# A third chunk's second group with its own place and bank, value rows added ahead of mean products, key copies ahead of maxima, and queries loaded later

## The chip, the cores and the metric

The kernel runs on one core of a Trainium2 chip. Its engines are TensorE (PE: products, with a separate queue of weight loads, PEld), VectorE (DVE), ScalarE (ACT), GpSimd (POOL) and SyncE (SP, which here only issues DMAs). The metric is the device time of one execution in microseconds (us), lower is better. A time is the median of several runs.

## The reference

Two layers in a row. The first is attention with a window: each query sees the keys less than 16 positions away, and beside them 24 block summaries (the maximum over each block of 32 keys, with the mean over the same 32 rows as its value). The second is a gated product with two up-projections and one down-projection.

```python
# q, k, v: (4, 8, 768, 64)   w_a, w_b: (512, 1536)   w_out: (1536, 512)
k_sum = k.reshape(B, H, nb, 32, D).max(axis=3)
v_sum = v.reshape(B, H, nb, 32, D).mean(axis=3)
scores_l = where(|i - j| < 16, scale * q @ k.T, -1e9)
scores_s = scale * q @ k_sum.T + log(32)
a = softmax(concat([scores_l, scores_s]))
x = (a @ concat([v, v_sum])) -> (3072, 512)
out = ((x @ w_a) * (x @ w_b)) @ w_out
```

## The kernel before

**Chunks, groups, items.** The 3072 rows are taken in 12 chunks of 256 (three per batch element), a chunk in two groups of 128 rows. For a group the kernel forms scores against 128 key columns per head (`scores`, L561), softmax, a transposition of the probabilities (`transposes`, L664) and the product with the values (`products`, L701), which is split into a high and a low part, `x` (L720 on ACT, L723 on DVE). An item (L937) is one chunk `u` and one block `f` of 128 of the 1536 hidden columns: 24 up-products into `h` (L932), four short operations on ACT and DVE (L949, L952, L954, L957), and 6 down-products into `o` (L968). There are 144 items. The first two chunks' items are interleaved, `(0,0) (0,1) (1,0) (0,2) (1,1) ...`, so that each block of weights is used twice while the weights are being prepared; from the third chunk on, the chunks follow one another.

**Weights.** The weights arrive as 36 raw parts, two to a pair `j` (0 to 17, tile `W{j}`), and `convert(j)` (L266) turns each into a high and a low part: per half of a pair ACT scales (L289) into bank `c0`, DVE runs three steps (L297, L304, L310) that use banks `c0` and `c1`, ACT makes the high part (L342), and POOL makes the low part with a subtraction and an addition (L347, L353). Pair `j`'s raw parts are loaded once pair `j - 4` is converted (`done{j-4}`). The last four pairs work in three half spaces that are taken in turn (`slots`, L264).

**The first two chunks** (`first_attention`, L742) have ways of their own: the keys are transposed by PE into four banks (`first_keys`, L417), ACT copies each to `kT` in two parts (L433 low, L435 high), DVE takes the block maxima (L443), POOL spreads them (`summaries`, L409). The block means of the values come from PE with a matrix of 1/32 (`means`, L822): six loaded pieces with two adjacent rows in each partition, two products for each piece.

**The third chunk** (`FILL`, attention(2), L856) is put between the conversions by three `yield`s. It shares `c0` and `c1` with them: `begin(0)` (query transposition L881, scores) comes after pair 9, `begin(1)` after pair 17. Both its groups put the transposed probabilities in `pbuf` (`pt`) and the value product in `c0`. Both use the same value rows `vbuf`, loaded by `bring`.

**Order.** Nothing is issued by hand. `Work.add` notes for each operation its engine, a rank, a guessed duration, and the keys that it reads and writes; `emit` (L50) plays the list against guessed times and issues, for the engine that is free first, the operation of lowest rank among those that are ready. The result is one fixed order for each engine, SP's loads included. Each engine works its order off one by one: what waits holds all behind it. Ranks: 0 for steps of an item on ACT and DVE, 1 for the first chunk, 2.3 for the second, `2 + j/4` for conversions, 5 for the third chunk, 5.5 for the next batch's keys, 6 for the rest.

**Spaces.** `S0` and `S1` hold 128x2048 each. Besides the conversions, `S0.0` and `S0.1` stage output rows, `S0.2` and `S0.3` hold the value sums of the next batch (`prep_values`, L497), `S1.0` and `S1.1` the value rows for them, `S1.2` and `S1.3` keys (`prep_keys`, L455).

Of the kernel before, what the change touches and what calls it, by code (L numbers as in the profile page):

```python
# [15 lines left out]
ALU = mybir.AluOpType  # L16
# [68 lines left out]
def attention_moe(  # L85
# [10 lines left out]
    nc = tc.nc  # L96
    B, H, S, D = q.shape
    P = 128
# [12 lines left out]
    CV = 512  # L111
    NW = 3 * NF // 2
    AHEAD = (7, 9, 17)
    FILL = 2

    const = ctx.enter_context(tc.tile_pool(name="const", bufs=1))
# [78 lines left out]
    for j in (*range(8, 13), *range(NW - 3, NW)):  # L195
        spaces[f"W{j}"] = wp.tile([P, 2048], F32, tag=f"W{j}", name=f"space{j}")

    kins = [kin, spaces["S1"][:, 2 * CV : 2 * CV + S + 32]]

    def slot(space, i):  # L200
# [12 lines left out]
    def act(rank, takes, reads, writes, fn):  # L213
        work.add("ACT", rank, takes, 0.08, reads, writes, fn)
# [46 lines left out]
            "SP", rank, 0.45, 524.0, [f"done{j - 4}"] if j > 3 else [], writes, fn, rate=340  # L261
        )

    slots = [("S0", 0), ("S0", 2), ("S1", 2)]  # L264

    def convert(j):  # L266
        rank = CONVERT + j / 4
        rk = [f"raw{2 * j}", f"raw{2 * j + 1}"]

        if j < NW - 4:  # L270
# [146 lines left out]
    def first_keys():  # L417
        n = P // BLK
        for i in range(S // P):
            x, key = spot(i // 2)  # L420
            x, key = x[:, i % 2 * 512 : (i % 2 + 1) * 512], key[i % 2]
            load(
                i, 262.0, 215, (), [key], x.rearrange("p (h d) -> p h d", d=D),
                heads(k[0, :, i * P : (i + 1) * P, :]),
            )
            bk = ("c0", "c1", "o2", "o3")[i % 4]
            pe(FIRST, 0.85, [key], [bk], lambda bk=bk, x=x: turn(bank[bk], x))
            c0 = PER * i

            def put(lo, bk=bk, c0=c0):  # L430
                tr = bank[bk].rearrange("p (c x) -> p c x", x=P)
                if lo:
                    nc.scalar.copy(out=kT[:, :, c0 + 16 : c0 + WIN], in_=tr[:, :, : WIN - 16])  # L433
                else:
                    nc.scalar.copy(  # L435
                        out=kT[:, :, c0 + P : c0 + PER + 16], in_=tr[:, :, WIN - 16 :]
                    )

            act(FIRST, 0.43, [bk], [f"kTl{i}"], lambda put=put: put(True))
            act(FIRST, 0.33, [bk], [f"kTh{i}"], lambda put=put: put(False))  # L440
            dve(
                FIRST, 0.6, [bk], [f"ksi{i}"],
                lambda bk=bk, i=i: nc.vector.tensor_reduce(  # L443
                    out=ks[:, :, i * n : (i + 1) * n],
                    in_=bank[bk].rearrange("p (c n x) -> p c n x", n=n, x=BLK),
                    axis=AX.X, op=ALU.max,
                ),
            )
        for c in range(NP):
            work.add("-", 0, 0, 0, [f"ksi{i}" for i in range(6)], [f"ks{c}"], lambda: None)  # L450
            reads = [f"kT{x}{i}" for i in range(6) for x in "lh"]
            work.add("-", 0, 0, 0, reads, [f"kT{c}k"], lambda: None)
            summaries(FIRST, c)

    def prep_keys(b):  # L455
# [91 lines left out]
    def load_values(b, t, vw, keys, rank):  # L547
        row = t * P
        skip = 16 if t == 0 else 0
        end = min(row + P + 16, S)  # L550
        for i, (e, r0, lo, hi) in enumerate((
            (0, skip, row - 16 + skip, row + 80),
            (1, 0, row + 48, row + 80),
            (1, 64, row + 80, end),
        )):
            load(
                rank, 2.1 * (hi - lo), 215, (), [keys[i]], vw[e][r0 : r0 + hi - lo],
                heads(v[b, :, lo:hi, :]),
            )

# [103 lines left out]
    def transposes(u, t, s, sk, banks, diag=None):  # L664
        rank = rank_of(u)
        if u < FILL:
            d, dk = diag

            def turned(h):
                for c in range(NP):  # L670
                    nc.tensor.matmul(
                        bank[banks[h]][:, c * P : (c + 1) * P], s[h][:, c, :], d[:, h, c, :],
                        start=True, stop=True,
                    )

            for h in range(2):
                pe(
                    -1, 0.85, [f"{sk[h]}{c}" for c in range(NP)] + dk[h], [banks[h]],
                    lambda h=h: turned(h),
                )  # L680
                act(
                    rank, 0.6, [banks[h]], dk[h],
                    lambda h=h: nc.scalar.copy(
                        out=d[:, h], in_=bank[banks[h]].rearrange("p (c x) -> p c x", x=P)
                    ),
                )
            return
        sv = sbuf.rearrange("p h c x -> p (h c) x")
        pv = pbuf.rearrange("p h c x -> p (h c) x")


        for i, kb in enumerate(((0, 1, 3), (1, 2, 3), (0, 1, 2), (1, 2, 3))):
            qs = slice(32 * i, 32 * (i + 1))
            for j in kb:
                js = slice(32 * j, 32 * (j + 1))
                dve(
                    rank, 0.45, sk, [f"pt{i}{j}"],
                    lambda js=js, qs=qs: nc.vector.transpose(out=pv[js, :, qs], in_=sv[qs, :, js]),  # L698
                )

# [36 lines left out]
    SK = ["s0", "s1"]  # L737
    PT = [f"pt{i}{j}" for i in range(4) for j in range(4)]

    PD = (pbuf, [[x for x in PT if (x[2] in "01") == (h == 0)] for h in range(2)])  # L740

    def first_attention():  # L742
# [78 lines left out]

        def means(n):  # L822
            g, i = n // 3, n % 3
            for y in range(2):
                nc.tensor.matmul(
                    bank["h0"][:, g * 256 : (g + 1) * 256], mean[:, 16 - 8 * i : 16 - 8 * i + P],
                    vin[n][0][:, :, y * D : (y + 1) * D],
                    start=(i == y == 0), stop=(i == 2 and y == 1),
                )

        for n in range(6):
            pe(FIRST + 0.5, 1.0, [vin[n][1], mk], ["h0"], lambda n=n: means(n))
        for e, r0 in ((0, WIN), (1, 32)):
            rows = slice(r0, r0 + 32)
            act(
# [20 lines left out]
    def attention(u):  # L856
# [1 line left out]
        b, r = u // NR, u % NR  # L858
        rank = rank_of(u)

        banks, vbank = [["c0", "c1"]] * 2, ["c0"] * 2
        if u > FILL:
            banks, vbank = [["c0", "c1"], ["o2", "o3"]], ["c0", "o2"]
        if r == 0:
# [2 lines left out]
        t0 = G * r  # L867
        qk = []
        for c in range(NP):
            qk += blocks(98, f"qin.{c}", qin[:, c, :], q, b, c, r * CH)  # L870

        def bring(i):
            load_values(b, t0 + i, vbuf, VK[:3], 97)
# [14 lines left out]
            transposes(u, t0 + i, s0, SK, banks[i])  # L888

        def end(i):  # L890
            return u, t0 + i, vbuf, VK, vbank[i]

        if u == FILL:

            yield
            bring(0)
            begin(0)
            turned(0)
            yield
            begin(1)  # L900
            yield
            values(*end(0))
            bring(1)
            turned(1)
            values(*end(1))
        elif u == FILL + 1:
            for i in range(G):
                bring(i)
                begin(i)
                turned(i)  # L910
                values(*end(i))
        else:

            for i in range(G):
                begin(i)
                bring(i)
                turned(i)
                lead.append(products(*end(i)))
# [128 lines left out]
```

## Time and profile before

| | |
|---|---|
| Median of 3 runs | 704.68 us (703.55 to 706.06) |
| Profiled execution | 704.12 us, span 702.4 us |
| Mean granted TensorE clock | 0.998 |
| Busy share of the span | PE 97%, PEld 89%, DVE 62%, ACT 36%, POOL 26% |
| Chain that ended last, by engine | PE 79%, DVE 7%, POOL 7%, issue 3%, ACT 2%, DMA 2% |
| HBM | 47.12 MB read, 6.29 MB written |

The span runs from the first to the last instruction; the execution's time has a little around it. A row of the timeline reads: start in us, length in us, engine, line of the kernel, operation, output<-input, shapes, count, and in brackets the idle time of the engine ahead of it with what ended it. A row of the table by stretches reads: the stretch and its length, then for each engine its busy time and (count), then PE's granted clock, the busy share of the DMA engines, and GB/s. `SPq` rows are DMA issues. A row of waits reads: engine and line that waited, for whom, total us, times, longest. Shares of busy time are averages over stretches with different limits, so they say little on a change to one stretch.

### The profile page before, as it was taken

How to read it: one execution, taken by the hardware profiler on the slowest of the kernel's cores; microseconds unless marked ns; L12 is line 12 of the kernel's file. 1: busy time of each engine (PE TensorE's matmuls, PEld its weight loads, DVE VectorE, ACT ScalarE, POOL GpSimd, SP SyncE). 2: the span in 40 equal slices, each digit the busy share in tenths (PEclk: the TensorE clock that was granted, in tenths of full speed). 3: DMA queues.
4: the chain of work that ended last, by engine and by line, in shares of the span. 5: the costliest groups of instructions: out<-in, count | busy, mean ns of one | idle time of the engine just before them, and what ended most of it. 6: DMA issues, size and time to landing. Idle time of an engine off the chain costs nothing.

```text
span 702.4 us, 15093 instructions
## 1 busy us (share of the span) xinstructions
PE 682.8 (97%) x6000; PEld 626.4 (89%) x6000; DVE 436.4 (62%) x988; ACT 252.4 (36%) x795; POOL 181.3 (26%) x219
## 2 busy tenths in 40 slices
PE   6888999999999999999999999999999999999997
PEld 3778999988999999999999999999999999999996
DVE  2898999797767777666763776762762662311221
ACT  2976574533333314332332323332331431211211
POOL 4378976852433521130110101110110110000000
PEclk9999999999999999999999999999999999999999
DMA  9979773076233335220300330310310100000000
GB/s 229 265 173 309 267 168 126 6 152 145 64 89 96 83 79 107 50 56 19 82 8 17 69 68 2 87 25 1 83 24 1 54 21 1 31 1 1 31 1 31
DMA packets 154943, 54.84 MB, mean 78 GB/s; under 512 B 132456, under 2 KB 147816, under 8 KB 154872
## 3 DMA queue, kind: packets, MB, share of 16 engines
q1 hardware_dynamic: 154872, 53.88, 31.5%
q8 instruction: 47, 0.77, 0.5%
q14 instruction: 24, 0.20, 0.1%
HBM read 47.12 MB, written 6.29 MB: 76 GB/s over the span
## 4 chain that ended last, share of the span: by engine, by line
PE 79%; DVE 7%; POOL 7%; issue 3%; ACT 2%; DMA 2%; SPq 0%; POOLq 0%; ACTq 0%; DVEq 0%
PE h L932 48%; PE o L968 24%; POOL w L353 3%; POOL S L347 2%; DVE c L304 2%; PE o L712 1%; PE c L712 1%; PE o L583 1%; PE c L583 1%; DVE space L297 1%; POOL space L347 1%; DVE space L310 1%; DMA raw<-in_moe_w_b_dram 1%; ACT s L628 1%; DVE ksum L443 1%
## 5 line engine op out<-in xcount | busy, mean ns | idle before, releaser
L932 PEld LDWEIGHTS h<-x,w 128*128 128x128 f32 x3456 | 416.0, 189 | 14.0 <-DVE x L723 2.2
L932 PE MATMUL h<-x,w 128*128 128x256 f32 x3456 | 419.4, 278 | 1.9 <-DVE x L723 1.7
L952 DVE TENSOR_TENSOR h<-h,g 128x256 f32<-128x256 f32 x144 | 62.2, 432 | 164.9 <-ACT g L949 163.2
L968 PE MATMUL o<-w,gh 128*128 128x512 f32 x576 | 157.8, 396 | 1.3 <-ACT gh L954 1.2
L949 ACT COPY g<-h 128x256 f32<-128x256 f32 x144 | 53.8, 374 | 280.8 <-PE h L932 279.9
L968 PEld LDWEIGHTS o<-w,gh 128*128 128x128 f32 x576 | 98.8, 188 | 18.6 <-ACT gh L954 2.3
L698 DVE STREAM_TRANSPOSE pt<-s 32x256 f32<-32x256 f32 x240 | 104.6, 436 | 8.7 <-POOL s L658 4.5
L658 POOL TENSOR_TENSOR s<-s,nml 128x512 f32<-128x512 f32 x40 | 41.6, 1042 | 257.0 <-DVE nml L643 255.5
L968 PE MATMUL o<-w,gl 128*128 128x512 f32 x288 | 90.1, 394 | 0.0
L957 DVE TENSOR_TENSOR gl<-h,gh 128x256 fp32r<-128x256 f32 x144 | 60.7, 422 | 31.6 <-ACT gh L954 30.2
L628 ACT ACTIVATE s<-s,nml 128x128 f32<-128x128 f32 x160 | 62.7, 398 | 43.3 <-DVE nml L616 43.3
L954 ACT CAST gh<-h 128x256 fp32r<-128x256 f32 x144 | 53.6, 372 | 67.6 <-DVE h L952 67.3
L968 PEld LDWEIGHTS o<-w,gl 128*128 128x128 f32 x288 | 53.8, 188 | 11.9 <-issue 0.3
L513 POOL TENSOR_TENSOR S<-S 96x512 f32<-96x512 f32 (+3 forms) x48 | 33.6, 699 | 39.1 <-DMA S<-in_v_dram 30.7
L347 POOL TENSOR_TENSOR space<-space,w 128x1024 f32<-128x1024 f32 (+1 forms) x13 | 26.7, 2056 | 18.8 <-ACT w L342 13.9
L628 ACT ACTIVATION_READ_ACCUMULATOR s<-s,nml 128x1 f32 x160 | 31.1, 194 | 0.0
L289 ACT ACTIVATE c<-raw 128x512 f32<-128x512 f32 x36 | 23.2, 644 | 13.2 <-DVE S L297 5.1
L353 POOL TENSOR_TENSOR w<-space 128x1024 fp32r<-128x1024 f32 (+1 forms) x13 | 26.8, 2059 | 0.9
L637 DVE TENSOR_SCALAR nml<-nml 128x4 f32<-128x4 f32 x40 | 9.8, 244 | 26.9 <-ACT s L628 26.9
L616 DVE TENSOR_REDUCE nml<-s 128x4 f32<-128x512 f32 x40 | 25.4, 669 | 0.0
L409 POOL COPY kT<-ksum 128x144 f32<-128x144 f32 x16 | 4.7, 308 | 61.5 <-DVE ksum L491 54.7
L347 POOL TENSOR_TENSOR S<-S,w 128x512 f32<-128x512 f32 (+1 forms) x11 | 17.6, 1598 | 9.7 <-ACT w L342 9.6
(100 smaller groups left out, 454.2 us busy)
## 6 DMA issues: line engine op xcount, KB each, us to landing
raw<-in_moe_w_a_dram SPq DMA_DIRECT2D x12, 512.0 KB
raw<-in_moe_w_b_dram SPq DMA_DIRECT2D x12, 512.0 KB
raw<-in_moe_w_out_dram SPq DMA_DIRECT2D x12, 512.0 KB
out_dram<-S SPq DMA_DIRECT2D x24, 256.0 KB
qin<-in_q_dram SPq DMA_DIRECT2D x160, 32.0 KB
S<-in_v_dram SPq DMA_DIRECT2D x24, 192.0 KB
vw<-in_v_dram SPq DMA_DIRECT2D x18, 192.0 KB
kin<-in_k_dram SPq DMA_DIRECT2D x24, 100.0 KB
```

Of the source, the lines that this page charges most:

```text
L347: lambda ms=ms, f8=f8: nc.gpsimd.tensor_tensor(out=f8, in0=f8, in1=parted(0)[:, ms].bitcast(F32), op=ALU.subtract),
L353: lambda ms=ms, f8=f8, p8=p8: nc.gpsimd.tensor_tensor(out=parted(1)[:, ms], in0=f8, in1=p8, op=ALU.add),
L513: lambda: nc.gpsimd.tensor_tensor(out=out, in0=i0, in1=i1, op=ALU.add),
L628: lambda h=h, c=c, sums=sums: nc.scalar.activation(s[h][:, c, :], x[h][:, c, :], AF.Exp, bias=m[:, 0, h, c : c + 1], scale=1.0, accum_out= ...
L658: lambda h=h, r=r: nc.gpsimd.tensor_tensor(out=s[h], in0=s[h], in1=r[:, :, None].broadcast_to([P, NP, P]), op=ALU.mult,),
L698: lambda js=js, qs=qs: nc.vector.transpose(out=pv[js, :, qs], in_=sv[qs, :, js]),
L932: nc.tensor.matmul(ps, w[:, c, part, :], x[xpart][:, c, :], start=(i == 0), stop=(i == n - 1))
L949: act(CHAIN, 0.38, [hk], [gk], lambda: nc.scalar.copy(out=g, in_=pa))
L952: lambda: nc.vector.tensor_tensor(out=pa, in0=pb, in1=g, op=ALU.mult),
L954: act(CHAIN, 0.41, [hk], [ghk], lambda: nc.scalar.copy(out=gh, in_=pa))
L957: lambda: nc.vector.tensor_tensor(out=gl, in0=pa, in1=gh.bitcast(F32), op=ALU.subtract),
L968: nc.tensor.matmul(bank[ok[j]], (gh if first else gl)[:, js], w[:, :, part, :], start=(f == 0 and first and part == 0), stop=(f == NF - 1 ...
```

## The change

1. `first_keys`: the two copies of a chunk of keys become one step of ACT, and DVE's maximum reads that step's key too, so it comes behind both copies.
2. `means`: POOL adds the two adjacent value rows of each piece in place, and PE takes one product for each piece instead of two.
3. The third chunk's query loads wait for `done4`.
4. The rank of `convert(j)` is `2 + j/6`. The three half spaces of the last four pairs are `S1.0`, `S0.0`, `S1.2` instead of `S0.0`, `S0.2`, `S1.2`.
5. The third chunk's second group puts its transposed probabilities in `S0.2` and `S0.3` (`pown`, cleared by POOL first) and its value product in `c1`; its transposes are entered ahead of the first group's value product, with rank 5, which is also the rank that the third chunk has.
6. The guessed rate of the value loads is 150 instead of 215; this changes only what `emit` plays with.

```diff
+    TURNS = 5
...
+    pown = spaces["S0"][:, 2 * CV :].rearrange("p (h c x) -> p h c x", h=2, x=P)
...
-    slots = [("S0", 0), ("S0", 2), ("S1", 2)]
+    slots = [("S1", 0), ("S0", 0), ("S1", 2)]
     def convert(j):
-        rank = CONVERT + j / 4
+        rank = CONVERT + j / 6
...
     # first_keys
-            act(FIRST, 0.43, [bk], [f"kTl{i}"], lambda put=put: put(True))
-            act(FIRST, 0.33, [bk], [f"kTh{i}"], lambda put=put: put(False))
+            act(FIRST, 0.75, [bk], [f"kT{i}"], put)
             dve(
-                FIRST, 0.6, [bk], [f"ksi{i}"],
+                FIRST, 0.6, [bk, f"kT{i}"], [f"ksi{i}"],
...
     # load_values
-                rank, 2.1 * (hi - lo), 215, (), [keys[i]], vw[e][r0 : r0 + hi - lo],
+                rank, 2.1 * (hi - lo), 150, (), [keys[i]], vw[e][r0 : r0 + hi - lo],
...
     # transposes
-        pv = pbuf.rearrange("p h c x -> p (h c) x")
+        own = u == FILL and t % G == 1
+        dst, key = (pown, "pu") if own else (pbuf, "pt")
+        pv = dst.rearrange("p h c x -> p (h c) x")
+        rank = TURNS if own else rank
...
-                    rank, 0.45, sk, [f"pt{i}{j}"],
+                    rank, 0.45, sk + ["S0.2"] * own, [f"{key}{i}{j}"],
...
     # first_attention
         def means(n):
             g, i = n // 3, n % 3
-            for y in range(2):
-                nc.tensor.matmul(
-                    bank["h0"][:, g * 256 : (g + 1) * 256], mean[:, 16 - 8 * i : 16 - 8 * i + P],
-                    vin[n][0][:, :, y * D : (y + 1) * D],
-                    start=(i == y == 0), stop=(i == 2 and y == 1),
-                )
+            nc.tensor.matmul(
+                bank["h0"][:, g * 256 : (g + 1) * 256], mean[:, 16 - 8 * i : 16 - 8 * i + P],
+                vin[n][0][:, :, :D], start=(i == 0), stop=(i == 2),
+            )
         for n in range(6):
-            pe(FIRST + 0.5, 1.0, [vin[n][1], mk], ["h0"], lambda n=n: means(n))
+            x, key = vin[n]
+            pool(
+                FIRST, 0.7, [], [key],
+                lambda x=x: nc.gpsimd.tensor_tensor(
+                    out=x[:, :, :D], in0=x[:, :, :D], in1=x[:, :, D:], op=ALU.add
+                ),
+            )
+            pe(FIRST + 0.5, 0.5, [key, mk], ["h0"], lambda n=n: means(n))
...
     # attention(u)
-        banks, vbank = [["c0", "c1"]] * 2, ["c0"] * 2
+        banks, vbank = [["c0", "c1"]] * 2, ["c0", "c1"] if u == FILL else ["c0"] * 2
...
-            qk += blocks(98, f"qin.{c}", qin[:, c, :], q, b, c, r * CH)
+            qk += blocks(98, f"qin.{c}", qin[:, c, :], q, b, c, r * CH, ["done4"] if u == FILL else ())
...
         def end(i):
-            return u, t0 + i, vbuf, VK, vbank[i]
+            pt = (pown, [PU, ["S0.2", "S0.3"]]) if u == FILL and i else None
+            return u, t0 + i, vbuf, VK, vbank[i], pt
...
             begin(1)
+            pool(rank, 0.9, (), ["S0.2", "S0.3"], lambda: nc.gpsimd.memset(pown, 0.0))
+            turned(1)
             yield
             values(*end(0))
             bring(1)
-            turned(1)
             values(*end(1))
```

More of the change, by code (lines that the diff above doesn't have):

```diff
@@ L428, in first_keys, with put @@
             c0 = PER * i
-            def put(lo, bk=bk, c0=c0):
+            def put(bk=bk, c0=c0):
                 tr = bank[bk].rearrange("p (c x) -> p c x", x=P)
[L432 to L436, printed above, removed]
-                    )
-            act(FIRST, 0.43, [bk], [f"kTl{i}"], lambda put=put: put(True))
-            act(FIRST, 0.33, [bk], [f"kTh{i}"], lambda put=put: put(False))
+                nc.scalar.copy(out=kT[:, :, c0 + 16 : c0 + WIN], in_=tr[:, :, : WIN - 16])
+                nc.scalar.copy(
+                    out=kT[:, :, c0 + P : c0 + PER + 16], in_=tr[:, :, WIN - 16 :]
+                )
+            act(FIRST, 0.75, [bk], [f"kT{i}"], put)
             dve(
-                FIRST, 0.6, [bk], [f"ksi{i}"],
+                FIRST, 0.6, [bk, f"kT{i}"], [f"ksi{i}"],
                 lambda bk=bk, i=i: nc.vector.tensor_reduce(
@@ L450, in first_keys @@
             work.add("-", 0, 0, 0, [f"ksi{i}" for i in range(6)], [f"ks{c}"], lambda: None)
-            reads = [f"kT{x}{i}" for i in range(6) for x in "lh"]
-            work.add("-", 0, 0, 0, reads, [f"kT{c}k"], lambda: None)
+            work.add("-", 0, 0, 0, [f"kT{i}" for i in range(6)], [f"kT{c}k"], lambda: None)
             summaries(FIRST, c)
@@ L738, in attention_moe @@
     PT = [f"pt{i}{j}" for i in range(4) for j in range(4)]
+    PU = [f"pu{i}{j}" for i in range(4) for j in range(4)]
     PD = (pbuf, [[x for x in PT if (x[2] in "01") == (h == 0)] for h in range(2)])
@@ L823, in means @@
             g, i = n // 3, n % 3
-            for y in range(2):
-                nc.tensor.matmul(
-                    bank["h0"][:, g * 256 : (g + 1) * 256], mean[:, 16 - 8 * i : 16 - 8 * i + P],
-                    vin[n][0][:, :, y * D : (y + 1) * D],
-                    start=(i == y == 0), stop=(i == 2 and y == 1),
-                )
-        for n in range(6):
-            pe(FIRST + 0.5, 1.0, [vin[n][1], mk], ["h0"], lambda n=n: means(n))
+            nc.tensor.matmul(
+                bank["h0"][:, g * 256 : (g + 1) * 256], mean[:, 16 - 8 * i : 16 - 8 * i + P],
+                vin[n][0][:, :, :D], start=(i == 0), stop=(i == 2),
+            )
+        for n in range(6):
+            x, key = vin[n]
[4 more added lines that the diff above has]
+                ),
+            )
+            pe(FIRST + 0.5, 0.5, [key, mk], ["h0"], lambda n=n: means(n))
         for e, r0 in ((0, WIN), (1, 32)):
```

## The prediction

> **What bounds the kernel now.** I read the page first (PE is busy nearly throughout), then the busy time of each engine in five stretches cut where the work changes: the first scores start at 18.32, the first expert products at 37.08, the second chunk's at 60.12, the third chunk's at 160.90.
>
> ```profile
> core 0: us, PE busy (x) PEld busy (x) DVE busy (x) ACT busy (x) POOL busy (x), PEclk, DMA share, GB/s
> 0.00:18.32 18.32, 10.64 (x41) 6.29 (x41) 5.12 (x8) 5.92 (x15) 9.05 (x57) 1.00 1.00 232
> 18.32:37.08 18.76, 17.55 (x229) 14.25 (x229) 16.49 (x32) 17.41 (x53) 7.20 (x8) 1.00 1.09 269
> 37.08:60.12 23.04, 19.80 (x197) 16.98 (x193) 20.21 (x41) 16.62 (x52) 16.23 (x11) 0.93 0.80 201
> 60.12:160.90 100.78, 97.61 (x788) 89.11 (x788) 93.45 (x184) 51.99 (x123) 76.73 (x48) 1.00 0.59 161
> 160.90:702.40 541.50, 537.24 (x4751) 499.76 (x4751) 301.17 (x727) 160.45 (x556) 72.05 (x97) 1.00 0.20 46
> ```
>
> After 160.90 PE is busy for 537.24 of 541.50 us: that stretch is PE's own work, and the change leaves it alone. So the time is the moment when the third chunk's products start, plus a constant 541.5, and only the first 160.9 us can move. In them PE stands idle for 7.68, 1.21, 3.24 and 3.17 us (length less busy), 15.3 in all. In the first stretch PE waits for keys. In the next two ACT and DVE are nearly full (17.41 and 16.49 of 18.76; 20.21 of 23.04 on DVE), so a chain of attention steps sets the pace; in the fourth PE and DVE (93.45 of 100.78) are both close to full.
>
> The chain in the first stretch is one of keys. Its rows in order of time, beginning with the first of six chunks of keys:
>
> ```profile
> 9.14 0.43 ACT L433 COPY kT<-c 128x320 f32<-128x320 f32 x1 [7.05 <-PE c L374]
> ...
> 9.60 0.69 DVE L443 TENSOR_REDUCE ksum<-c 128x16 f32<-128x512 f32 x1 [7.59 <-ACT kT L433]
> ...
> 10.32 0.32 ACT L435 COPY kT<-c 128x192 f32<-128x192 f32 x1 [0.76 <-DVE ksum L443]
> ...
> 16.63 0.69 DVE L443 TENSOR_REDUCE ksum<-c 128x16 f32<-128x512 f32 x1 [0.71 <-ACT kT L433]
> ...
> 17.38 1.05 POOL L409 COPY kT<-ksum 128x144 f32<-128x144 f32 x4 [6.80 <-DVE ksum L443]
> ```
>
> ACT's low copy, DVE's maximum and ACT's high copy take turns on one bank, so from the first maximum to the sixth a chunk costs (16.63 - 9.60) / 5 = 1.41 us, and POOL's key sums, then the scores at 18.32, wait for the sixth.
>
> The second thing is what holds up the second chunk, from the queue of SP, ACT, PE and POOL:
>
> ```profile
> 30.50 12.73 SPq L225 DMA_DIRECT2D qin<-in_q_dram  x16
> ...
> 52.86 0.61 SPq L254 DMA_DIRECT2D raw<-in_moe_w_b_dram  x1
> 54.23 1.04 PE L712 MATMUL o<-pt,vw 128*64 128x64 f32 x28 [0.66 <-DMA vw<-in_v_dram]
> 55.69 1.03 PE L712 MATMUL o<-space,space 128*64 128x64 f32 x28 [0.21 <-DMA space<-in_v_dram]
> 58.04 0.63 ACT L289 ACTIVATE c<-raw 128x512 f32<-128x512 f32 x1 [2.16 <-DMA raw<-in_moe_w_b_dram]
> 58.61 0.58 ACT L720 CAST x<-o 128x512 fp32r<-128x512 f32 x1
> 60.22 2.41 POOL L347 TENSOR_TENSOR space<-space,w 128x1024 f32<-128x1024 f32 x1 [2.43 <-ACT w L342]
> ```
>
> SP spends 12.73 us issuing the third chunk's queries, which nobody reads before 82.69 (below), and the raw weights stand behind them. One comes so late that ACT waits 2.16 us for it, with the second chunk's cast (L720, 58.61) queued behind that wait.
>
> The third thing is the end of the fourth stretch: what PE waited for in it, and the rows around the last conversions and the third chunk's second group.
>
> ```profile
> PE h L932 <- DVE x L723: 1.7, 2, 1.3
> PE o L968 <- ACT gh L954: 1.2, 2, 0.6
> ...
> PE h L932 <- POOL w L353: 0.2, 1, 0.2
> ...
> 82.69 0.70 DVE L881 STREAM_TRANSPOSE qT<-qin 128x512 f32<-128x512 f32 x1
> 109.84 1.77 DVE L698 STREAM_TRANSPOSE pt<-s 32x256 f32<-32x256 f32 x4
> 116.67 0.69 DVE L297 TENSOR_SCALAR S<-c 128x512 int32<-128x512 int32 x1
> 122.06 1.30 POOL L347 TENSOR_TENSOR S<-S,w 128x512 f32<-128x512 f32 x1 [6.04 <-ACT w L342]
> 141.44 1.15 PE L712 MATMUL c<-pt,vw 128*64 128x64 f32 x32 [0.35 <-DVE s L608]
> 146.70 1.04 POOL L658 TENSOR_TENSOR s<-s,nml 128x512 f32<-128x512 f32 x1 [0.40 <-DVE nml L643]
> 148.20 0.87 DVE L698 STREAM_TRANSPOSE pt<-s 32x256 f32<-32x256 f32 x2
> ```
>
> **The change, part by part.** Amounts are on the start of the third chunk's products; minus is a gain.
>
> *Key copies ahead of maxima.* Both copies now precede the maximum, so ACT copies chunk i+1 while DVE reduces chunk i. A chunk then costs the larger of 0.69 (DVE) and 0.43 + 0.32 = 0.75 (ACT): the six end near 9.14 + 6 x 0.75 + 0.69 = 14.3 instead of 16.63 + 0.69 = 17.32, a gain of 3.0. PE could follow by no more than 7.68 less the 4.47 us that it waits for its first mask, 3.2. DMA is full in both early stretches (share 1.00 and 1.09), so queries, values and raw weights need not come earlier with it: between 0 and -3.0 I take -2.5, nearer the chain's end because every wait in these rows is for ACT or DVE and none for a load.
>
> *Value rows added by POOL.* Twelve of 24 mean products go, and six additions of 128x256 come on POOL.
>
> ```profile
> 20.31 3.72 PE L825 MATMUL h<-space,space 128*128 128x256 f32 x16
> 29.72 1.28 POOL L347 TENSOR_TENSOR space<-space,w 128x512 f32<-128x512 f32 x1 [11.28 <-ACT w L342]
> L513 POOL TENSOR_TENSOR S<-S 96x256 f32<-96x256 f32 x3 | 2.2, 733 | 0.2
> ```
>
> PE is rid of 12 x 3.72 / 16 = 2.8 us, POOL gets 6 x 0.73 = 4.4 us inside an idle stretch of 11.28. PE is not what paces this stretch, so I take 0. Ends: -2.8, if PE were the pace, and +1.0, if POOL waits for a late value load with the key sums (1.05, 17.38) queued behind it. Without that cover the 4.4 would come in front of the first weight subtraction at 29.72.
>
> *Third queries loaded late.* They now wait for the conversion of weight pair 4, and SP goes straight on to raw weights and value rows. What goes: ACT's 2.16 wait, of which the cast at 58.61 gets 58.61 - (55.69 + 1.03) = 1.9 less about 0.2 of handing over, 1.7; and the value waits of 0.66 + 0.21. Together -2.5; ends 0 and the stretch's whole idle time, -3.24. The 16 issues (12.73 us) go into gaps between raw loads; DVE needs them by the time that takes 82.69 now. If they are later than that, DVE's in-order queue holds the conversions: rival 2.
>
> *Conversion rank j/6 instead of j/4.* Pairs 13 to 17 now go ahead of the third chunk's work on DVE and POOL. Before, twelve transposes and little else ran from 109.84 to 116.67 while pair 14 waited, and POOL idled for 6.04; so the last conversions come some 6 us earlier. By itself that saves only the 0.2 wait for L353, but without it PE could not keep an earlier start, since it meets the conversions there with no slack. The price: pairs 2 to 4 now rank level with or ahead of the second chunk's second group, and one conversion step of 0.69 in front of a reduction costs that: +0.7 (0 to +2.1 for three).
>
> *Own place and bank for the second group.* Its transposes began at 148.20, just after POOL's scaling (146.70 + 1.04 = 147.74), long after the first group's product had read the old place (141.44 + 1.15). So the own place removes no wait that is there: 0. What helps is that the scores behind it come with the conversions, 6 us earlier, and then x is no longer late at 160.90: -1.0 of the 1.3 in the first wait row (0 to -2.5 with the 1.2 for gh). The place is paid for by a clearing on POOL (a 128x512 operation is 1.28, so at most 2.6, in gaps) and by the value sums of the next batch, whose half of the space is held until the second group's product; these feed PE late:
>
> ```profile
> 189.83 1.15 PE L712 MATMUL c<-pt,vw 128*64 128x64 f32 x32
> ```
>
> That product serves the fourth chunk, after the third's twelve items; their up-products alone take 12 x 2.91 (106.18, below) = 35 us, so it is not needed before 160.9 + 35 = 195.8, and 6 us late costs 0.
>
> The other half of the space, S1.0, now takes part in the last conversions, so the next batch's value loads and POOL's first sums over them move behind the last conversion:
>
> ```profile
> 48.40 2.62 POOL L513 TENSOR_TENSOR S<-S 96x512 f32<-96x512 f32 x3 [0.46 <-DMA S<-in_v_dram]
> ```
>
> POOL is rid of 2.62 us there and has them later, in gaps: 0. The changed rate of the value loads only moves the planner's guess: 0.
>
> *Sum*: -2.5 + 0 - 2.5 + 0.7 - 1.0 = -5.3. The profiled execution took 704.12 us (span 702.4 and 1.72 around it): 698.8. The median of the runs is 704.68, 0.56 above it, so I predict 699.4.
>
> **A rule that speaks against it.** Where PE waited 2.02 us, its granted clock fell, and 24 products took longer than the 2.91 of the row at 106.18 below:
>
> ```profile
> 46.03 1.13 PE L671 MATMUL o<-pt,s 128*128 128x128 f32 x8 [2.02 <-ACT space L628]
> 46.91 4.61 PE L932 MATMUL h<-x,w 128*128 128x256 f32 x24
> 48.00:50.00 2.00, 2.00 (x12) 2.00 (x11) 1.90 (x6) 1.27 (x7) 1.52 (x2) 0.50 1.04 370
> ```
>
> That slow spell cost 4.61 - 2.91 = 1.7. The change thins PE's work by 2.8 us in the stretch before, so a second spell can come there: the sum would be -3.6, which is 701.1. The Trainium skill ("TensorE: Matmul & The Clock Gate", Part 1) says that the clock is halved after an idle window of about 3.4 us that runs freely and does not follow the kernel. By it the spell may come, go or stay by chance of position; the 0.50 row agrees with the half, no row here shows the window.
>
> **The rivals.**
> 1. *Conversions stay the pace.* PE arrives earlier at 60 but must wait for weights: POOL runs pair after pair at 2.41 + 2.41 us, and gets only the 2.43 wait at 60.22 back. Against it: pair 14's 6 us. Gain 2.0: 702.7.
> 2. *Queries too late: slower.* In order behind the raw loads, which SP issues until 75.5, the sixteen would be issued by 75.5 + 12.7 = 88.2 and land 1 to 5 us later (the raw load of 52.86 was there at 58.04, in a full DMA; I take 2 for these small ones): 90, and DVE's L881, in place at 82.69, would hold everything behind it 7.5 us. Part of that is covered by weights in hand (pair 11's end against its use):
>
> ```profile
> 100.12 2.41 POOL L353 TENSOR_TENSOR w<-S 128x1024 fp32r<-128x1024 f32 x1
> ...
> 106.18 2.91 PE L932 MATMUL h<-x,w 128*128 128x256 f32 x24
> ...
> 75.10 0.43 SPq L254 DMA_DIRECT2D raw<-in_moe_w_a_dram  x1
> ```
>
>  106.18 - 102.53 = 3.7. It decides from a hold of some 4 us on; at 7.5 PE ends 3.8 later: 708.5. For it: SP took 0.8 us for each, far more than a raw load's 0.43. Against: raw loads now start up to 12.7 us sooner and leave gaps.
> 3. *Nothing moves*: DMA, full until 37, paces the start and the queries' place only swaps waits: 704.7.
> 4. *All idle goes*: the second stretch's 1.2, the third's 3.24 with the 1.7 of clock, 2.5 of the fourth and 3.0 of the first, less 2 that stay: -9.6, 695.
>
> **How the numbers follow.** Forecast 0.50 (own range 697 to 702), the second slow spell 0.05, rival 1 0.20, rival 2 0.12, rival 3 0.05, rival 4 0.08. Range 694.5 to 704.5: it leaves out rival 2, half of rival 3 and the tail of rival 4, under 0.2. A difference under 0.3%, 2.1 us, can't be told from none. Faster than 702.6: 0.50 + 0.08 + 0.03 + half of rival 1, 0.71. Same: the other half, rival 3 and the rest of the spell, 0.17. Slower: 0.12.
>
> **What would show it.** Right: maxima 0.7 apart instead of 1.4, first scores near 15; 12 mean products; no ACT wait on a raw load near 58 and the second chunk's products near 55; no pause of POOL near 116; the third chunk's products near 155.6, and the stretch after them 541.5 long. Wrong: DVE waiting before L881 with idle POOL behind it, PE waiting for L353 between 60 and 150, or new idle time of PE after 160.

## The result, and the profile after

| | before | after |
|---|---|---|
| Median | 704.14 us (703.55 to 706.06, 4 runs) | 697.05 us (696.66 to 698.4, 4 runs) |
| Ratio, 95% interval | | 0.9896 [0.9879, 0.9914] |
| Profiled execution | 704.12 us, span 702.4 | 698.4 us, span 696.7 |

The change makes the kernel 7.1 us faster; 5.3 was forecast (699.4). A second set of runs of the same kernel gave 696.88 us, 0.9912 [0.9898, 0.9926], its profiled execution a span of 694.6.

Two marks between the start and the end order what follows: the first product of the fifth item (96 up-products lie before it), and the first product of the third chunk's first item (576 before it). Here is busy time between the marks in the kernel before (columns: stretch and length, busy time of each engine with its instructions, PE's granted clock, DMA share, GB/s).

```profile
core 0: us, PE busy (x) PEld busy (x) DVE busy (x) ACT busy (x) POOL busy (x), PEclk, DMA share, GB/s
0.00:67.88 67.88, 55.11 (x515) 44.18 (x515) 49.37 (x92) 44.38 (x125) 39.99 (x78) 0.97 0.97 240
67.88:159.17 91.29, 90.10 (x735) 82.26 (x734) 84.16 (x168) 47.12 (x114) 69.23 (x45) 1.00 0.54 149
159.17:702.40 543.23, 537.62 (x4752) 499.94 (x4752) 302.90 (x730) 160.88 (x557) 72.05 (x97) 1.00 0.20 46
```

And the same in the changed kernel:

```profile
0.00:64.34 64.34, 53.24 (x508) 41.78 (x509) 49.15 (x94) 44.85 (x126) 42.59 (x81) 0.97 1.08 256
64.34:153.01 88.67, 88.67 (x730) 81.95 (x728) 83.34 (x164) 46.90 (x112) 67.99 (x42) 1.00 0.54 145
153.01:696.70 543.69, 538.00 (x4753) 499.92 (x4751) 302.63 (x732) 161.27 (x557) 75.81 (x104) 1.00 0.21 47
```

The first stretch is 3.54 us shorter, the second 2.62, the third 0.46 longer: 5.70 in all, which is the difference of the two executions. One set of six down-products (1.5 us: two sets start at 61.34 and 62.85 in the changed kernel) has moved from the second stretch into the first. Like for like the first is thus 5.0 shorter, and the second 1.1, about the 1.19 us (91.29 - 90.10) that PE stood idle there; now it is busy for all 88.67.

The rows of the changed kernel that answer to those shown of before, in order of time (start, length, engine, line, operation, output<-input, count, idle time before and its releaser):

```profile
9.11 1.29 DVE L442 TENSOR_REDUCE ksum<-c 128x16 f32<-128x512 f32 x2 [7.10 <-ACT kT L435]
...
11.51 1.28 DVE L442 TENSOR_REDUCE ksum<-c 128x16 f32<-128x512 f32 x2
...
14.32 1.10 PE L581 MATMUL o<-kT,qT 64*64 64x128 f32 x32 [0.34 <-ACT qT L809]
17.13 0.72 POOL L836 TENSOR_TENSOR space<-space 128x256 f32<-128x256 f32 x1 [3.21 <-DMA space<-in_v_dram]
...
36.96 3.10 PE L942 MATMUL h<-x,w 128*128 128x256 f32 x24
...
43.63 0.34 PE L714 MATMUL o<-pt,vw 128*64 128x64 f32 x4 [1.42 <-DMA vw<-in_v_dram]
...
46.14 4.09 PE L942 MATMUL h<-x,w 128*128 128x256 f32 x24
...
55.90 5.61 PE L942 MATMUL h<-x,w 128*128 128x256 f32 x48
63.03 5.73 SPq L227 DMA_DIRECT2D qin<-in_q_dram  x8
78.51 0.70 DVE L889 STREAM_TRANSPOSE qT<-qin 128x512 f32<-128x512 f32 x1
132.07 1.30 POOL L355 TENSOR_TENSOR w<-S 128x512 fp32r<-128x512 f32 x1
```

The maxima follow one another in (11.51 - 9.11) / 4 = 0.60 us instead of 1.41, and the first scores start at 14.32 instead of 18.32. Yet the first up-products start at 36.96, only 0.12 earlier: POOL waits 3.21 for value rows ahead of its additions (L836), PE on the way 1.5 for these additions and 1.9 for DVE (L648), and the 4.0 us are used up. They come back at the second chunk's products, 55.90 instead of 59.54. The third queries are issued until 63.03 + 5.73 = 68.8 and read at 78.51, so they are not late. The row at 132.07 is the last step of the last conversion; in the kernel before it is this one, 11.5 us later:

```profile
143.58 1.29 POOL L353 TENSOR_TENSOR w<-S 128x512 fp32r<-128x512 f32 x1
```

One new wait of PE comes after the third chunk's start (the row of PE's waits after 170: engine and line, for whom, total, times, longest; then the two places in the timeline):

```profile
PE c L714 <- DMA vw<-S: 1.4, 2, 1.0
```

```profile
195.34 0.34 PE L714 MATMUL c<-pt,vw 128*64 128x64 f32 x4 [1.02 <-DMA vw<-S]
196.09 1.04 PE L714 MATMUL c<-pt,vw 128*64 128x64 f32 x28 [0.41 <-DMA vw<-S]
```

That is the product at the value sums which the prediction had put at "6 us late costs 0".

### The profile page after: what moved, and what is told of

It is laid out like the page before. It is cut to its first block, busy times and chain, and to the rows that moved or that the text cites. A ratio compares the mean times of both kernels' runs of the same rounds, so it can differ in the third digit from the quotient of the medians.

```text
span 696.7 us, 15098 instructions
## 1 busy us (share of the span) xinstructions
PE 679.9 (98%) x5988; PEld 623.6 (90%) x5988; DVE 435.1 (62%) x988; ACT 253.0 (36%) x795; POOL 186.4 (27%) x226
## 4 chain that ended last, share of the span: by engine, by line
PE 91%; DMA 3%; SPq 2%; DVE 1%; ACT 1%; POOL 1%; issue 1%; DVEq 0%; ACTq 0%; POOLq 0%
PE h L942 55%; PE o L978 28%; SPq L227 2%; PE o L714 2%; PE c L714 2%; PE c L581 2%; PE o L581 1%; DMA vw<-in_v_dram 1%; DMA space<-in_v_dram 1%; PE o L669 1%; DVE pt L700 1%; DMA S<-S 0%; POOL s L656 0%; DMA vw<-S 0%; SPq L256 0%
## 5 line engine op out<-in xcount | busy, mean ns | idle before, releaser
L700 DVE STREAM_TRANSPOSE pt<-s 32x256 f32<-32x256 f32 x228 | 99.4, 436 | 8.1 <-POOL s L656 2.4
```

## The experiments

Two theories were to be told apart. By the first, the parts add up: each gives its term of the sum, wherever the others are. By the second they are links of one chain: a lead that is won early is kept only where the later stages, the weights above all, can follow, so a part is worth little alone and much in company. Six kernels take one part out of the changed kernel, one mends it, and four put one or two parts into the kernel before. All are timed against the kernel before in five rounds.

The lead over the kernel before at each mark, from one profiled execution each (67.88, 159.17 and 702.4 less the kernel's own; at the fifth item 1.5 us are added for kernels marked *, which have done six down-products more by then; but for the twelve mean products, PE's work ahead of each mark is then the same in all), the ratio of the timed runs, and their clock (below):

| kernel | fifth item | third chunk | end | ratio [95%] | clock |
|---|---|---|---|---|---|
| changed * | 5.0 | 6.2 | 5.7 | 0.9896 [0.9879, 0.9914] |  |
| changed, again * | 6.3 | 7.7 | 7.8 | 0.9912 [0.9898, 0.9926] | +1.7 |
| less late queries | 2.3 | 4.4 | 6.8 | 0.9927 [0.9909, 0.9945] | -0.9 |
| less key copies * | 3.4 | 4.5 | 4.6 | 0.9939 [0.9924, 0.9955] | +3.0 |
| less additions * | 1.6 | 3.3 | 3.2 | 0.9957 [0.9941, 0.9974] | -1.1 |
| less rank | 5.2 | 2.6 | 2.3 | 0.9979 [0.9966, 0.9992] | +1.5 |
| less own place * | 2.8 | 4.2 | 3.3 | 0.9946 [0.9926, 0.9965] | 0.0 |
| less rate * | 3.0 | 5.1 | 6.9 | 0.9932 [0.9914, 0.995] | -0.5 |
| changed, sums apart * | 6.3 | 7.4 | 9.8 | 0.9885 [0.9867, 0.9903] | +1.2 |
| before + rank | 1.9 | 3.4 | 4.4 | 0.9945 [0.9925, 0.9964] | -0.2 |
| before + key copies | 1.0 | 0.7 | 0.5 | 1.0033 [1.0017, 1.0048] | -3.2 |
| before + additions | 0.4 | 0.5 | -2.5 | 1.0024 [1.001, 1.0038] | -1.1 |
| before + both | 0.7 | 0.7 | -2.7 | 1.0026 [1.0008, 1.0044] | -2.6 |

What a part is worth in company is the difference of its ratio to that of the changed kernel (0.9904, the mean of its two sets, for the first four; 0.9912, from the same chip, for the others) times 703.5 us; with intervals of about 0.0018 each way it is good to some 1.5 us.

The last column is the mean granted clock of the timed executions less that of the kernel before in the same set (0.9968 to 0.9975), in thousandths; for the first set the clocks of the kernel before are not on record. An estimate from it: one thousandth of some 700 us is 0.7 us of PE's work, at most, since the mean also counts the end of an execution, where PE has nothing left to do. Held against the +1.7 of the changed kernel, time at a lower clock can then make up all that the late queries and the rate are worth (1.8 of 1.6 and 1.5 of 1.4), about half of the additions and of the own place (2.0 of 3.7 and 1.2 of 2.4), and next to nothing of the key copies and the rank.

**The changed kernel again**, beside the kernels of the second set.

> The changed kernel itself once more, beside the three that follow. Its profile showed two paces of the up-products, 114.4 and 117.8 ns from one start to the next, the slow one between 80 and 130 us and in parts of 150 to 350 us; over about 105 us of slow stretches that is 3 us. If the pace belongs to the kernel, the slow stretches come again in the same places and the time is 697; if it belongs to the execution, they lie elsewhere or are gone.

696.88 us (696.35 to 698.21). The two profiles of one kernel differ by 2.1 us of span, 1.3 of it ahead of the fifth item, where the value rows came earlier in this one:

```profile
42.67 0.66 PE L714 MATMUL o<-pt,vw 128*64 128x64 f32 x4 [0.40 <-DMA vw<-in_v_dram]
43.53 1.03 PE L714 MATMUL o<-pt,vw 128*64 128x64 f32 x28 [0.20 <-DMA vw<-in_v_dram]
44.50 3.31 PE L942 MATMUL h<-x,w 128*128 128x256 f32 x24
```

PE waited 0.6 us here, against 1.42 + 0.67 at 43.63 in the first profile, and its clock did not drop behind it (3.31 against 4.09 at 46.14, where the first profile has 3.42 us at half the clock, shown further on). So a microsecond or two between single profiles is no sign of anything.

**Queries not late.**

```diff
-            qk += blocks(98, f"qin.{c}", qin[:, c, :], q, b, c, r * CH, ["done4"] if u == FILL else ())
+            qk += blocks(98, f"qin.{c}", qin[:, c, :], q, b, c, r * CH)
```

> The changed kernel, with the third chunk's queries loaded as early as before (no wait for pair 4's conversion). Theory A (the prediction's terms): this edit carries 2.5 us, so 699.5 against 697.0 for the changed kernel. Theory B (read from the trace of the changed kernel, in which the first products start at 36.96, only 0.1 us earlier than before, and the second chunk's at 55.90, 3.6 to 4.2 earlier): nearly all of the early gain is this edit's, so +4, about 701, with ACT again waiting for a raw load near 55 to 58. Theory C (DMA only swaps its order): 697.

698.31 us (697.28 to 699.71): the late queries are worth 1.6. SP issues them in one run again, with the second chunk's value rows behind (SP's queue), and PE takes the first chunk's second item ahead of the value product, where it waits for weights (PE's rows):

```profile
30.13 13.58 SPq L227 DMA_DIRECT2D qin<-in_q_dram  x16
...
44.78 1.68 SPq L227 DMA_DIRECT2D vw<-in_v_dram  x3
...
46.37 1.58 PE L942 MATMUL h<-x,w 128*128 128x256 f32 x10 [2.49 <-POOL w L355]
```

ACT waits for a raw load again too, 1.66 us at 47.51, and PE's clock is at half for 6.8 us (0.75, 0.50 and 0.84 in 47 to 48, 48 to 54 and 54 to 55). That PE's own wait comes from the same 13 us of SP, by the order planned around them, is read from the queues and was not tested by itself.

**Key copies around the maxima again**, as in the kernel before.

```diff
-            act(FIRST, 0.75, [bk], [f"kT{i}"], put)
+            act(FIRST, 0.43, [bk], [f"kTl{i}"], lambda put=put: put(True))
+            act(FIRST, 0.33, [bk], [f"kTh{i}"], lambda put=put: put(False))
             dve(
-                FIRST, 0.6, [bk, f"kT{i}"], [f"ksi{i}"],
+                FIRST, 0.6, [bk], [f"ksi{i}"],
```

> The changed kernel, with the key copies split around the maxima as before. Theory A: +2.5, 699.5, since the first scores move back from 14.3 to about 18. Theory B: the scores move back by those 4 us, but the first products stay within 0.5 us of 36.96, because value loads, ACT and DVE set the pace between 14 and 37: 697 to 697.5.

699.59 us (699.07 to 699.76): worth 2.5. The first products start at 39.95 instead of 36.96 and 37.05, and the lead is 1.6 to 2.9 less at the first mark and 1.7 to 3.2 at the second: the lost time is lost for good.

**Two mean products, no additions.**

```diff
-            pool(FIRST, 0.7, [], [key],
...
-            pe(FIRST + 0.5, 0.5, [key, mk], ["h0"], lambda n=n: means(n))
+            pe(FIRST + 0.5, 1.0, [vin[n][1], mk], ["h0"], lambda n=n: means(n))
```

> The changed kernel, with two mean products for each piece and no additions on POOL, as before. Theory A (the term was 0): 697. Theory B: PE has 2.8 us more work, yet in the stretch to 37 it is idle for about as long, and PE no longer waits 1.5 us for POOL's additions: 696 to 697.5. Rival: PE's work counts in full, 699.8.

700.78 us (699.45 to 702.97): worth 3.7, where the prediction had 0. PE's rows in the stretch that the prediction gave to ACT and DVE:

```profile
17.38 3.72 PE L828 MATMUL h<-space,space 128*128 128x256 f32 x16
...
28.96 0.66 PE L376 MATMUL o<-ident,space 128*128 128x128 f32 x4
32.09 1.98 PE L569 MATMUL o<-mask,ident 128*128 128x512 f32 x4 [2.47 <-ACT qT L809]
...
39.07 3.02 PE L937 MATMUL h<-x,w 128*128 128x256 f32 x24
```

Between 17.38 and 29.62 PE waits only 0.5 us. With twice the mean products in its queue it ends the transposition of queries (L376) at 29.62 instead of 27.84; ACT's copy of them, for which PE waits at 32.09, comes behind that, and the first products start at 39.07, 2.1 later. Once the scores start early, PE's own work is part of the pace here. More is lost behind it: PE waits 2.01 for x ahead of the row at 48.10, with its clock at half for 3.4 us.

**Rank j/4.**

```diff
-        rank = CONVERT + j / 6
+        rank = CONVERT + j / 4
```

> The changed kernel, with the conversions' rank 2 + j/4 as before. Theory A: the edit's own gain is 0.2 less 0.7 of price, but it is what lets PE keep its lead; without it PE meets the last conversions near 122 as before and all idle time of the fourth stretch returns: +3 to +4, 700 to 701, with PE waiting for L355 near 120 to 145. Rival (conversions are early enough by the earlier raw loads alone): 697 to 697.5.

702.39 us (701.8 to 703.95): worth 5.3, the most of all parts. The stretches (first two of three):

```profile
0.00:62.72 62.72, 50.89 (x503) 39.60 (x504) 48.20 (x92) 43.74 (x125) 40.94 (x80) 1.00 1.11 253
62.72:156.57 93.85, 91.22 (x736) 82.48 (x734) 85.83 (x167) 47.66 (x115) 69.92 (x44) 1.00 0.54 142
```

At the fifth item this kernel leads by 5.2 us, as the changed one does (5.0 and 6.3), and then it loses half: 93.85 in the second stretch, 2.6 more than in the kernel before, and all of that idle time (93.85 - 91.22), of which the changed kernel has none. The table shows the same in every row: with j/6 the lead grows from the first mark to the second by 1.1 to 2.2, with j/4 it stays within 0.3 or falls. PE's waits up to 170:

```profile
PE o L978 <- ACT gh L964: 1.9, 4, 1.0
PE o L978 <- POOL w L355: 1.6, 1, 1.6
```

**Shared place.** The second group goes back to `pbuf` and `c0`, and the half spaces of the last pairs to the old order, without the clearing.

```diff
-    slots = [("S1", 0), ("S0", 0), ("S1", 2)]
+    slots = [("S0", 0), ("S0", 2), ("S1", 2)]
...
-        own = u == FILL and t % G == 1
+        own = False
```

> The changed kernel, with the third chunk's second group in the first one's place and bank again, the half spaces of the last conversions and the place of its transposes in the list as before. Theory A (the prediction: the own place removes no wait): 0 for the place, and the next batch's value sums are no longer held until the second group's product, so PE's wait of 1.4 for them near 195 goes: 695.5 to 697. Rival (the second group waits for the first group's product): +2 to +3, 699 to 700, with PE waiting for x of L725 near 155.

698.79 us (697.7 to 701.5): worth 2.4. In the profiled execution (700.86, one of the two longest of six) it is lost ahead of the fifth item, long before the second group's place is used, and PE waits only 0.6 for x up to the third chunk. With `S1.0` free again, the next batch's value loads come early and stand in front of the second chunk's (SP's queue, then PE).

```profile
30.50 0.97 SPq L227 DMA_DIRECT2D S<-in_v_dram  x2
...
44.10 0.34 PE L714 MATMUL o<-pt,vw 128*64 128x64 f32 x4 [1.79 <-DMA vw<-in_v_dram]
45.30 1.76 PE L714 MATMUL o<-pt,vw 128*64 128x64 f32 x28 [0.86 <-DMA vw<-in_v_dram]
46.99 4.94 PE L941 MATMUL h<-x,w 128*128 128x256 f32 x24
```

Up to the row at 44.10 PE's list is that of the changed kernel; its wait for value rows is 2.65 us instead of 0.6 (second profile) or 2.09 (first), and 24 products behind it take 4.94 instead of 3.31 or 4.09, at half the clock: it lasts 6.8 us here (granted clock 0.66, 0.50 and 0.93 in 44 to 45, 45 to 51 and 51 to 52), twice as long as in the first profile of the changed kernel. How the loss divides between loads and clock is open.

**Rate 215.**

```diff
-                rank, 2.1 * (hi - lo), 150, (), [keys[i]], vw[e][r0 : r0 + hi - lo],
+                rank, 2.1 * (hi - lo), 215, (), [keys[i]], vw[e][r0 : r0 + hi - lo],
```

> The changed kernel, with the guessed rate of the value loads at 215 as before. Theory A: the guess alone moves nothing, 697 within 0.5. Rival: PE's order puts the second chunk's value product ahead of work that is ready, so that it waits longer than now (2.1 us near 44) for value rows: 698 to 700.

698.53 us (696.7 to 699.88): 1.4 by the ratios, with intervals that overlap, so its size isn't settled. The order differs from the changed kernel's all the same: the first products start at 36.01, and the lead at the fifth item is 3.0.

**Value sums apart.** The means of the next batch go to a tile of their own instead of `S0.3`, which the second group's own place holds.

```diff
+    vmt = sb([P, D], "vm")
...
-        vm, pk = slot("S0", 3)
-        vm = vm[: 4 * NS, :D]
+        vm, pk = vmt[: 4 * NS, :], "vm"
```

> The changed kernel, with the value sums of a batch gathered in a small tile of their own (256 bytes in each partition) instead of S0.3, so that they do not wait for the third chunk's second group. POOL waited 8.59 us for that product before a sum (150.30), and PE later 1.4 us for the sums' load near 195. Theory: the sums come 4 to 9 us earlier and the 1.4 goes, 695.6. Rival (PE has the same work and only waits elsewhere): 697.

694.54 us (694.21 to 697.17), the fastest kernel here, 1.9 below the changed one on the same chip; the intervals still touch. The third stretch:

```profile
151.76:692.60 540.84, 536.64 (x4753) 499.35 (x4751) 302.58 (x732) 160.58 (x557) 72.18 (x98) 1.00 0.20 46
```

It is 2.9 shorter than in the first profile of the changed kernel and 2.3 shorter than in the second (543.12), and PE has no wait in it. The waits taken away were 1.4 and 1.2; the rest is in PE's busy time.

**One or two parts alone, in the kernel before.** First the rank:

```diff
-        rank = CONVERT + j / 4
+        rank = CONVERT + j / 6
```

> The kernel before, with the conversions' rank 2 + j/6 and nothing else. Taking this edit out of the changed kernel cost 5 to 6 us. Theory A (edits work only together: PE has no lead that the earlier conversions could protect): 0 to -1, 702.5 to 703.5. Rival (a gain of its own): -3 to -5, 699, with the fourth stretch's 3.17 us of idle time gone.

699.74 us (699.57 to 700.05): half of the whole gain and more, from one number. The first two stretches, and PE's only wait between the second chunk's and the third chunk's products:

```profile
0.00:65.94 65.94, 53.90 (x514) 43.43 (x515) 49.45 (x93) 44.47 (x126) 39.57 (x77) 0.97 1.02 240
65.94:155.74 89.80, 88.88 (x736) 82.11 (x735) 82.76 (x167) 46.99 (x113) 70.36 (x46) 1.00 0.57 158
```

```profile
PE c L712 <- DVE x L723: 0.9, 1, 0.9
```

In the kernel before there stood 1.7 for x, 1.2 for gh and 0.2 for weights. So the rank also takes most of the waits for x and gh away, of which the prediction had booked 1.0 under the own place and the rest at nothing; the "price" of pairs 2 to 4 didn't come: the lead at the fifth item is 1.9. The last conversion's last step comes 10.2 us earlier (133.41 against 143.58).

The key copies alone, and the additions alone (points 1 and 2 of the change, the reverse of the two diffs above), and both together:

> The kernel before, with the key copies ahead of the maxima and nothing else. Taking it out of the changed kernel cost 2.4 to 3.2 us. The prediction's own term: -2.5, 701. Theory A (edits work only together): the first scores come 3 to 4 us sooner, but PE then has all 24 mean products and the first products start less than 1 us sooner; the queries still hold SP, so 703 to 703.7.

> The kernel before, with POOL's additions and 12 mean products and nothing else. Taking it out of the changed kernel cost 3.7 to 4.4 us. The prediction's term: 0, 703.5. Rival (PE's 2.8 us count in full by themselves): 700.8.

> The kernel before, with the key copies ahead of the maxima and the mean products halved, nothing else. If the two help each other, more than the sum of the two alone: first products at 34 to 35 instead of 37.1, and 700 to 701.5. If the value loads and raw loads set the pace up to 37, the first products stay at 36.5 to 37 and the time is 703.

705.96 us (703.33 to 707.98), 705.7 (703.34 to 706.66) and 705.96 (703.35 to 708.14): slower than before, by 2.3, 1.7 and 1.8 us. With the key copies alone the first scores start at 15.00 instead of 18.32, and the first products at 38.07, a microsecond later than before. PE's rows show what took the place of the keys:

```profile
31.39 0.34 PE L708 MATMUL h<-space,space 128*64 128x64 f32 x4 [1.33 <-DMA space<-in_v_dram]
32.54 1.50 PE L708 MATMUL h<-space,space 128*64 128x64 f32 x28 [0.81 <-DMA space<-in_v_dram]
```

Value rows, from a DMA that is full until 37. In this execution PE's clock is also at half here, where the kernel before has such a spell after 47:

```profile
33.00:36.00 3.00, 3.00 (x23) 1.85 (x21) 1.84 (x3) 1.92 (x4) 1.32 (x2) 0.50 1.06 356
```

With both, the small lead of 0.7 is lost late. PE's row, DVE's and POOL's around it:

```profile
225.66 3.05 POOL L509 TENSOR_TENSOR S<-S 96x512 f32<-96x512 f32 x4 [4.64 <-DMA S<-in_v_dram]
...
231.70 0.43 DVE L694 STREAM_TRANSPOSE pt<-s 32x256 f32<-32x256 f32 x1 [2.94 <-POOL s L654]
...
238.41 1.03 PE L708 MATMUL o<-pt,vw 128*64 128x64 f32 x28 [1.99 <-DVE pt L694]
```

In POOL's fixed order four additions of value rows (3.05 us, late from the DMA) stand ahead of two scalings; DVE's transposition waits 2.94 for the second, PE 1.99 for DVE. Soon behind the wait PE's clock is at half once more:

```profile
240.00:243.00 3.00, 3.00 (x25) 2.28 (x18) 2.01 (x4) 0.08 (x1) 2.60 (x6) 0.50 0.40 87
```

The additions alone show the same wait with 1.6, and a second spell at half the clock after the third chunk's first product (0.50 in 161 to 164, behind a wait of 1.3 for x). For the key copies alone the profile (703.65 us, near the lower end of its runs) has only 0.4 of the wait and one spell. Its median goes with the clock: three of its twelve executions, with 0.997 and 0.998, took 703.3 to 704.0 us, as the kernel before does, and the other nine, all but one with 0.990 to 0.994, took 705.3 to 708.0. By the estimate above the clock is worth up to 2.2, 0.8 and 1.8 of the 2.3, 1.7 and 1.8 us. Why these kernels have more of such spells was not tested.

The parts that were taken out sum to 1.6 + 2.5 + 3.7 + 5.3 + 2.4 + 1.4 = 16.9 us, the whole is worth 6.7 (0.9904). Two parts that are worth 2.5 and 3.7 in company cost about 2 us alone, of which the clock can be nearly all (key copies) or about half (additions). The first theory has fallen. The second holds for these two and not for the rank, which is worth 3.9 by itself.

## Why the prediction was right, and where it was not

The time (697.05 against 699.4), the direction and the place (the time up to the third chunk's first product; 159.17 - 153.01 = 6.2 against 5.3) were right. Of the signs announced, the maxima 0.7 apart (0.60), the first scores near 15 (14.32), the second chunk near 55 (55.90), POOL without its pause and the length of the last stretch within 0.5 us all came. (This is by the mark used here; the prediction's own, 160.90, stands behind the wait for x, and from it the start moved by 7.9 to 153.01, not to 155.6, and the last stretch grew by 2.2.) One sign of being wrong came too: new idle time of PE after 160, 1.4 us. The split was mostly wrong:

- *Keys, -2.5.* 2.5 in company, but +2.3 alone. The step that failed is "every wait in these rows is for ACT or DVE and none for a load": that is true of the rows of before, and the next thing to be late was a load. It named rival 3 for this ("DMA, full until 37"), which fits this part taken alone, but for the clock, which goes with most of the +2.3.
- *Means, 0.* 3.7 in company, good to 1.5 and in part by the clock, so at the lower end of -2.8 or beyond it. "PE is not what paces this stretch" was read off the idle time of a stretch whose start the change moves.
- *Late queries, -2.5.* 1.6: about right in size. By the queues the weights and value rows behind SP's 13 us were the reason; beside ACT's wait for a raw load (1.66) a wait of PE comes back (2.49) and a longer spell at half the clock, which the sum did not have.
- *Rank, -0.2 and a price of +0.7.* The worst term: 5.3 in company, 3.9 alone (0.0055 x 703.5). The prediction saw that the conversions come earlier (6 us foreseen, 11.5 measured, 10.2 with the rank alone) and called this a cover for the other gains, which the run with j/4 confirms: a lead of 5.2 shrinks to 2.6. That the wait for x goes with the earlier conversions it had seen too, but it booked this under the own place and left gh out of the sum. Its price, which was weighed against it, was not there; by the ranks only pairs 2 and 3 (2.33 and 2.5) come ahead of or level with the second chunk's second group (2.5), not pair 4.
- *Own place, 0 in itself and -1.0 with x.* 2.4 in company, but not for x, for which PE waits only 0.6 without the own place: by the loads that it pushes out of the full stretch, and by the clock behind them. The prediction named this move ("value loads and POOL's first sums over them move behind the last conversion") and put it at 0, counting POOL's 2.62 us and not the DMA.
- *Late value sums, 0.* 1.4 us of waiting, 1.9 by the run that takes the cause away. The product isn't needed until a chunk later, as the prediction said, but it stands at its place in PE's order and PE waits there.
- *Rate, 0.* 1.4, not settled.

Errors of both signs met: the large gain of rank and means that was left out went into what the other parts couldn't use without them. That the total came near is luck in part: 697.05 lies at the edge of the prediction's own range of 697 to 702, and is about as far from rival 4's 695 as from 699.4. Some 1.2 us of the gain (the +1.7 of the table) is a higher clock, which no term had. Rivals 1 and 2 did not come (no wait for weights after 56; queries issued 10 us ahead of their use). Rival 4 came in the second stretch, where no idle time is left, and not ahead of the first up-products.

In the changed kernel the clock spell was not added: it stayed, once, in the first profile of after, and was absent from the second; a second one came in the two kernels that put the additions into the kernel before. In the first profile the granted clock by stretches reads:

```profile
45.00:45.50 0.50, 0.50 (x16) 0.50 (x16) 0.50 (x3) 0.02 (x1) 0.50 (x1) 0.58 1.10 294
...
48.20:48.40 0.20, 0.20 (x3) 0.20 (x2) 0.20 (x2) 0.17 (x2) 0.00 (x0) 0.50 1.08 298
48.40:49.00 0.60, 0.60 (x7) 0.60 (x6) 0.43 (x1) 0.57 (x4) 0.00 (x0) 0.92 1.11 315
```

At 0.58 half the clock holds for 84% of 0.50 us, at 0.92 for 16% of 0.60, and 45.50 to 48.40 lies at 0.50: 0.42 + 2.90 + 0.10 = 3.42 us. The Trainium skill ("TensorE: Matmul & The Clock Gate", Part 1) gives a free-running window of 3413 ns at half the clock; length and half agree, and that one kernel has the spell in one execution and not in the next fits a window that doesn't follow the kernel. The fourteen traces agree: after their first 10 us they hold eleven such spells, nine of 3.41 us and two of 6.83, and within each trace all changes of the clock lie whole multiples of 3.413 us apart, to 2 ns. But the window ahead of a spell isn't idle, as the prediction's rule has it: PE was busy in 0.33 to 0.60 of it (0.39 ahead of 45.09 here), and its longest single wait here was 1.42 us.

What stays open: why the key copies alone bring more time at half the clock, and the sizes of the rate and the own place, which change the order in many places at once.

## What to carry to other kernels

In a kernel whose orders are fixed by a list, place marks on the bounding engine and read at each how much of a lead has arrived: a local chain that got 4.0 us shorter was worth nothing until the stages behind it (value rows, PE's own work, the conversions) were early too. So cost an edit in company and alone, and look at idle time in the stage where the lead has to be kept: there one rank was worth more than any of the three shortened chains. Before a few us are put down to a part, compare the granted clock of the executions: here it went with about half or all of what four of six parts seemed worth. A result "not needed until later" still stops an in-order engine at the place where its use stands in the list, and a transfer that an edit moves is to be costed on the DMA as well as on the engine behind it.

## What the runs showed of the hardware that was not expected

*Two paces of PE at full clock.* 24 up-products take 2.91 or 2.99 us, for tens of us at a time, with a granted clock of 1.00. Around 90 us, first in the first and then in the second profile of the same kernel:

```profile
89.09 2.99 PE L942 MATMUL h<-x,w 128*128 128x256 f32 x24
```

```profile
88.02 2.91 PE L942 MATMUL h<-x,w 128*128 128x256 f32 x24
```

From start to start that is 117.8 or 114.4 ns for a product. It changes where other products interrupt the items, differs between two executions of one kernel, and costs up to 1.9 us in a run (23 items of 24 products at 3.4 ns in the first profile); its cause is open.

*A small DVE operation held for a whole POOL operation.* DVE's and POOL's rows of the changed kernel:

```profile
112.91 1.45 DVE L635 TENSOR_SCALAR nml<-nml 128x4 f32<-128x4 f32 x1
116.99 1.25 DVE L635 TENSOR_SCALAR nml<-nml 128x4 f32<-128x4 f32 x1
...
113.38 0.96 POOL L910 MEMSET S<- 128x1024 f32 x1
116.93 1.29 POOL L349 TENSOR_TENSOR S<-S,w 128x512 f32<-128x512 f32 x1
```

512 elements take 1.45 and 1.25 us, and each ends within 0.02 us of the POOL operation (114.36 and 114.34; 118.24 and 118.22). The Trainium skill ("SBUF — State Buffer", SBUF: two separate sides) describes a port pair that the two engines lock against each other for a whole instruction, for DVE operations in a 2-port mode or with two inputs in SBUF; these rows agree with the lock, and no run here tells in which mode this operation, with one input, works.
